# A quarter of the first output rows, stored in whole rows over SP's and GpSimd's queues

## The chip, the cores and the metric

One core of a Trainium2 chip runs the kernel. The metric is the device time of one execution in microseconds, 171.88 us as the median of three runs before the change.

## What is computed

Linear attention without a softmax over 8 batches and 8 heads, a root-mean-square norm of its output, and a soft mixture of 8 experts over the 4608 tokens that come out:

```python
kv = np.einsum('bhsd,bhse->bhde', k, v)
out = np.einsum('bhsd,bhde->bhse', q, kv)
x = out / np.sqrt(np.mean(out * out, axis=-1, keepdims=True) + 1e-06) * g_norm   # as [4608, 512]
logits = x @ phi                                     # [4608, 32]
d = softmax of logits over the tokens;  slot_input = d.T @ x
for e in range(8): slot_out[e] = np.maximum(slot_input[e] @ w1[e], 0) @ w2[e]
return (softmax of logits over the slots) @ slot_out  # [4608, 512]
```

Everything is float32. The inputs are 62 MB, the output 9.4 MB.

## The kernel before

The kernel writes out its own order: every operation is recorded by the class `Order`, with the waits that its operands need, and emitted engine by engine in the order of the program. That is why nearly every row of the profile has one line, L214.

First k, v and q stream in and the attention output is made, token tile by token tile, while the sums over the tokens run along. Then the weights w1 and w2 of the eight experts stream in over the same memory (`arena`), and TensorE makes `expert_h` and `expert_y` as they come. All loads are issued by SP on one queue (q1 in the profile); the last load of weights is issued at 126.46 us.

The output is made in two halves (`hf`) of six chunks each. `output(hf, k, f)` makes chunk n = hf x 6 + k x 2 + f: TensorE multiplies, ScalarE copies one half of the chunk from PSUM into `arena`, VectorE the other half. A chunk is 128 partitions (rows, here) of 1536 floats, 6144 bytes each. `OUT_ROWS` says which chunks are stored together: 0 to 2, 3 to 5, 6 and 7, 8 to 11. The last three stores are one DMA each, over all 128 rows, issued by SP as soon as their last chunk is copied. The first three chunks are stored in pieces by `store_first`, along the table `FIRST`. An entry of it reads: issuing engine, first partition p0, step, number of rows n, length a of the outermost dimension of the destination, number c of pieces that a row is cut into, first chunk k0 and end k1. Each piece goes out as soon as chunk k1 - 1 is there:

- rows 1, 5, 9, ... (every fourth, 32 of them, "the quarter" below): chunk 0 over SP, 30 rows with an outer dimension of 5 (five DMA engines, six rows each) and two rows cut in three; chunk 1 over GpSimd's queue, 24 rows and 8 rows, with an outer dimension of 2 (two engines each); chunk 2 over SP together with rows 3, 7, ...
- rows 3, 7, 11, ...: chunks 0 and 1 over SP, rows of 12288 bytes on all 16 engines
- even rows: chunks 0 to 2 over SP, rows of 18432 bytes on all 16 engines

A DMA that GpSimd issues runs on its own queue, q0. `step_over(n)` is a small copy on that queue, of n rows of 32 bytes from an input into a scrap tile, `stepped`; nobody reads it. Before, there are two of them, of 7 and 6 rows (`STEPS`): the first ahead of the experts, the second between GpSimd's two stores.

The names that the prediction uses: `store_first` and its loop over `FIRST`, `step_over`, `output` with its calls of `store_first` and of the later stores, `load_w`.

Of the kernel before, what the change touches and what calls it, by code (L numbers as in the profile page):

```python
# [11 lines left out]
P = 128  # L12
# [40 lines left out]
OUT_AT = tuple(range(72, 144, 6))  # L53
OUT_ROWS = ((0, 1, 2), (3, 4, 5), (6, 7), (8, 9, 10, 11))
CHUNK = 4 * 12 * 32
FIRST = (
    ("sync", 1, 4, 30, 5, 1, 0, 1), ("sync", 121, 4, 2, 3, 3, 0, 1),
    ("gpsimd", 1, 4, 24, 2, 1, 1, 2), ("gpsimd", 97, 4, 8, 2, 1, 1, 2),
    ("sync", 3, 4, 32, 1, 1, 0, 2), ("sync", 0, 2, 64, 1, 1, 0, 3), ("sync", 1, 2, 64, 1, 1, 2, 3),
)  # L60
STEPS = (7, 6)
SHARED = (5, 11)
HEAD = 144
SCRATCH = 1024
# [212 lines left out]
def first_pieces(out):  # L277

    at = 0
    for _, p0, step, n, a, c, k0, k1 in FIRST:  # L280
        size = (k1 - k0) * CHUNK
        part = out[at : at + n * size]
        rows = part.reshape(n * c // a, a, size // c).swapaxes(0, 1)
        yield p0, step, n, k0, k1, rows.reshape(n, size)
        at += n * size


def soft_moe_linear_attention(nc, first_in, kv_in, q0_in, q1_in, kv4_in, kv5_in, t3_in, w_in, out):
# [12 lines left out]
    def place(at, n):  # L301
        return arena[:, HEAD + at * KB : HEAD + at * KB + n]
# [67 lines left out]
    stepped = const.tile([P, 16], F32, name="stepped")  # L370
# [35 lines left out]
    class Kv:  # L406
# [10 lines left out]
        def products(self, r):  # L417
            g, w = divmod(r, 2)
            main = kv_main(self.b, g).rearrange("p (r w c n) -> p r w c n", r=2, w=2, c=4)
            for c in range(4):  # L420
                for i in range(2):
                    lo = 64 * i
                    nc.tensor.matmul(
                        self.pkv[lo : lo + 64, w, g],
                        lhsT=main[:, w, 1, c, lo : lo + 64],
                        rhs=main[:, w, 0, c, lo : lo + 64],
                        start=c == 0 and (g == 0 or self.b == 0),
                        stop=False,
                    )
# [248 lines left out]
    ends = {starts[s + 1] - 1: s for s in range(len(STAGES))}  # L678
# [46 lines left out]
    for T in range(NT - 2):  # L725
# [3 lines left out]
        o = products(T)  # L729
# [143 lines left out]
    def expert_h(e):  # L873
        ph = ps.tile([P, 2, 512], F32, tag="m", name=f"ph{e}")[:, 0, :256]
        for c in range(4):
            for j in range(4):
                nc.tensor.matmul(
                    ph[32 * j : 32 * j + 32],
                    lhsT=sTe[:, (4 * e + c) * NS : (4 * e + c + 1) * NS],
                    rhs=w_block("w1", e, 4 * c + j),  # L880
                    start=c == 0,
                    stop=c == 3,
                )
        h = wk.tile([P, 256], F32, tag="part", name=f"h{e}", bufs=3)
        nc.scalar.activation(h, ph, AF.Relu, scale=rs)

        x = xts[(NT - 1 - e // 2) % NX].rearrange("p j n -> p (j n)")
        hTs[e] = x[:, e % 2 * 256 : e % 2 * 256 + 256].rearrange("p (c n) -> p c n", n=NS)
        nc.vector.transpose(out=hTs[e].rearrange("p c n -> p (c n)"), in_=h)
# [31 lines left out]
            nc.tensor.matmul(pz[f], lhsT=sel.rearrange("p a n -> p (a n)"), rhs=ys[hf][f], start=True, stop=True)  # L921
        zs[hf] = halves(f"z{hf}", pz)

    def step_over(n):
        ends = [x[:n, : 2 * w].rearrange("p (c n) -> p c n", c=2)[:, :, :4] for x, w in ((stepped, 8), (first_in, 64))]
        nc.gpsimd.dma_start(*ends)

    steps = list(STEPS[::-1])

    def store_first(n):  # L930
        at = 0
        for engine, p0, step, m, a, c, k0, k1 in FIRST:
            size = (k1 - k0) * CHUNK
            if k1 == n + 1:
                src = place(OUT_AT[k0], size)[p0 : p0 + step * (m - 1) + 1 : step]
                dst = out[:, at : at + m * size]
                if c > 1:
                    src = src.rearrange("p (c n) -> p c n", c=c)
                dst = dst.rearrange("o (b a n) -> (o a) b n", a=a, n=size // c)
                getattr(nc, engine).dma_start(dst, src)  # L940
                if engine == "gpsimd" and steps:
                    step_over(steps.pop())
            at += m * size

    def output(hf, k, f):
        z = zs[hf]
        n = (hf * NCH + k) * 2 + f
        at = OUT_AT[n]
        st = place(at, 4 * CT * NS).rearrange("p (a n) -> p a n", a=4)
        shared = n in SHARED  # L950
        for v in range(2):
            fourth = hf == 1 and (2 * n + v) % 4 == 3
            apart = shared and v == 1
            pots = [
                ps.tile([P, 2, 512], F32, tag="y" if y else "m", name=f"po{hf}_{k}_{f}_{v}_{i}", bufs=1 if y else None)
                for i, y in enumerate((False, fourth) if apart else (fourth,))
            ]
            for u in range(2):
                lo = 32 * (2 * v + u)
                po = pots[u if apart else 0]  # L960
                nc.tensor.matmul(
                    po[:, 0 if apart else u, : CT * NS].rearrange("p (g x) -> p g x", g=2),
                    lhsT=z[f][lo : lo + 32],
                    rhs=cT[k][lo : lo + 32],
                    start=True,
                    stop=True,
                )
            if apart:
                nc.vector.tensor_copy(out=st[:, 2], in_=pots[0][:, 0, : CT * NS])
                nc.scalar.copy(st[:, 3], pots[1][:, 0, : CT * NS])  # L970
            elif v == 0:
                nc.scalar.copy(st[:, 0:2], pots[0][:, :, : CT * NS])
            else:
                nc.vector.tensor_copy(out=st[:, 2:4], in_=pots[0][:, :, : CT * NS])
        if n <= OUT_ROWS[0][-1]:
            store_first(n)
        for row in OUT_ROWS[1:]:
            if row[-1] == n:
                lo, m = row[0] * 4 * CT * NS, len(row) * 4 * CT * NS
                nc.sync.dma_start(  # L980
                    out[:, lo * P : (lo + m) * P].rearrange("o (p n) -> (o p) n", p=P), place(OUT_AT[row[0]], m)
                )

    step_over(steps.pop())
    expert_h(0)
    load_w("w2", 3)
    expert_h(1)
# [23 lines left out]
    for k, f in chunks:  # L1011
        output(0, k, f)
# [4 lines left out]
    for k, f in chunks:  # L1017
        output(1, k, f)


def build_program():
    import concourse.bacc as bacc

    nc = bacc.Bacc("TRN2", target_bir_lowering=False, num_devices=1, dynamic_dma_scratch_size=SCRATCH)
    shapes = {
        "first": (P, HEAD + 2304), "kv": (4, P, TOK), "q0": (P, TOK), "q1": (P, 2048),
        "kv4": (P, 2560 + TOK), "kv5": (P, 2 * TOK), "t3": (P, 3 * TOK),
        "w": (1, 2 * NE * P * UNIT),
    }
    args = [nc.dram_tensor(f"in_{n}_dram", s, F32, kind="ExternalInput").ap() for n, s in shapes.items()]  # L1030
    args.append(nc.dram_tensor("out_0_dram", (1, 4 * NCH * P * 4 * CT * NS), F32, kind="ExternalOutput").ap())
    order = Order(nc)
    soft_moe_linear_attention(order, *args)
    order.emit()
    return nc
# [61 lines left out]
```

## Time and profile before

| | us |
|---|---|
| median of 3 runs | 171.88 (171.79 to 171.90) |
| the profiled execution, its own time | 172.04 |
| span of that execution, first to last instruction | 170.70 |
| TensorE busy | 151.3 (89%) |
| VectorE, ScalarE, GpSimd busy | 86.6, 89.0, 59.6 |
| the core's 16 DMA engines | 71.65 MB, 420 GB/s in the mean |

Times in the rows are counted from the start of the span. "DMA share" is the busy share of the 16 DMA engines, q1 is the queue that SP issues to, q0 the one that GpSimd issues to, and an issue's "us to landing" runs from its issue to the last of its engines' reports. A packet is one row or one piece of a row; the packet by which a DMA reports its end on an engine is one of 4 bytes. The execution moves as much data as the DMA engines can for most of its length.

### The profile page before, as it was taken

The numbers are of one execution on the slowest core, as the hardware profiler recorded it, in microseconds if no ns is written. First come the engines' busy times: TensorE is split into PE (matmuls) and PEld (weight loads), VectorE is DVE, ScalarE is ACT, GpSimd is POOL, SyncE is SP. The second block draws the span as 40 slices with busy tenths as digits, with TensorE's granted clock in tenths as the row PEclk, the third lists the DMA queues.
The fourth block names the chain that finished last, engine by engine and source line by source line (L and its number), as shares of the span: only waits on it lengthen the run. The fifth ranks groups of instructions, "written<-read, shape, count | busy, mean of one in ns | idle before, by whom it ended". The sixth has DMA issues, their size and how long they took to land.

```text
span 170.7 us, 4234 instructions
## 1 busy us (share of the span) xinstructions
PE 151.3 (89%) x1832; PEld 105.5 (62%) x1832; DVE 86.6 (51%) x185; ACT 89.0 (52%) x230; POOL 59.6 (35%) x73
## 2 busy tenths in 40 slices
PE   7989697989999899999899998989999989998700
PEld 3469576979778878897697674346665543345300
DVE  1122156284677266762946698823888137205700
ACT  3036576796975886859759864202223045205700
POOL 7000707638357745377382679500000004000000
PEclk9999999999999999999999999999999999699965
DMA  5999999999999999999999999999999999999988
GB/s 190 414 429 423 443 418 440 465 422 454 449 418 434 431 428 430 418 409 449 422 434 422 434 407 426 443 428 420 430 426 438 451 418 407 420 432 410 405 380 369
DMA packets 4365, 71.65 MB, mean 420 GB/s; under 512 B 790, under 2 KB 790, under 8 KB 922
## 3 DMA queue, kind: packets, MB, share of 16 engines
q1 hardware_dynamic: 3994, 71.18, 97.8%
q8 instruction: 14, 0.23, 0.5%
q0 software_dynamic: 352, 0.20, 0.4%
q14 instruction: 5, 0.04, 0.1%
HBM read 61.94 MB, written 9.44 MB: 418 GB/s over the span
## 4 chain that ended last, share of the span: by engine, by line
PE 59%; DMA 13%; ACT 12%; DVE 7%; SPq 2%; issue 1%
PE psum L214 59%; DMA arena<-in_kv_dram 13%; ACT bd L214 3%; ACT sq L214 3%; ACT xall L214 2%; SPq L214 2%; DVE arena L214 1%; DVE logits L214 1%; ACT arena L214 1%; DVE ms L214 1%; ACT part L214 1%; ACT d L214 1%; DVE part L214 1%; ACT r L214 1%; DVE acc L214 1%
## 5 line engine op out<-in xcount | busy, mean ns | idle before, releaser
L214 PE MATMUL psum<-bd,arena 128*128 128x192 f32 (+1 forms) x320 | 56.1, 335 | 1.9 <-ACT bd L214 1.5
L214 PEld LDWEIGHTS psum<-bd,arena 128*128 128x128 f32 (+1 forms) x320 | 45.4, 179 | 8.6 <-ACT bd L214 2.8
L214 DVE TENSOR_REDUCE ms<-sq 128x16 f32<-128x1024 f32 (+1 forms) x19 | 22.1, 1163 | 32.5 <-ACT sq L214 32.3
L214 POOL TENSOR_TENSOR part<-part,r 128x512 f32<-128x512 f32 x17 | 17.8, 1048 | 49.7 <-DVE r L214 49.7
L214 POOL TENSOR_TENSOR xall<-xall,r 128x512 f32<-128x512 f32 x34 | 34.7, 1042 | 0.0
L214 ACT ACTIVATE sq<-psum 128x512 f32<-128x512 f32 x36 | 21.5, 598 | 11.6 <-PE psum L214 11.3
L214 PEld LDWEIGHTS psum<-arena 128*64 128x64 f32 (+1 forms) x640 | 19.0, 137 | 8.3 <-DMA arena<-in_kv_dram 3.2
L214 PE MATMUL psum<-arena 128*64 128x64 f32 (+1 forms) x640 | 21.7, 226 | 2.2 <-DMA arena<-in_kv_dram 2.2
L214 ACT COPY xall<-psum 128x512 f32<-128x512 f32 x34 | 20.6, 606 | 0.0
L214 ACT COPY part<-psum 128x256 f32<-128x256 f32 (+1 forms) x38 | 13.6, 359 | 12.9 <-DVE part L214 11.7
L214 DVE TENSOR_REDUCE logits<-part 128x64 f32<-128x512 f32 (+1 forms) x18 | 17.8, 990 | 0.0
L214 PE MATMUL psum<-arena,xall 128*32 128x256 f32 x256 | 16.4, 411 | 0.0
L214 PE MATMUL psum<-logits,part 32*128 32x384 f32 x96 | 13.5, 524 | 1.5 <-ACT arena L214 0.7
L214 PEld LDWEIGHTS psum<-arena,xall 128*32 128x32 f32 x256 | 8.8, 118 | 7.2 <-issue 2.8
L214 ACT COPY arena<-psum 128x768 f32<-128x768 f32 (+1 forms) x14 | 10.2, 754 | 5.3 <-PE psum L214 5.2
L214 POOL DMA_DIRECT2D out_dram<-arena x2 | 1.2, 592 | 33.4 <-ACT arena L214 33.4
L214 PE MATMUL psum<-arena,sq 128*32 128x256 f32 x224 | 12.7, 379 | 0.2 <-DVE sq L214 0.2
L214 DVE COPY arena<-psum 128x768 f32<-128x768 f32 (+1 forms) x12 | 10.3, 888 | 4.7 <-PE psum L214 4.7
L214 PE MATMUL psum<-xall,d 128*32 128x258 f32 x144 | 10.8, 390 | 0.8 <-ACT d L214 0.8
L214 PEld LDWEIGHTS psum<-logits,part 32*128 32x128 f32 x96 | 6.3, 183 | 7.8 <-ACT arena L214 4.3
L214 ACT COPY bd<-psum 64x128 f32<-64x128 f32 (+1 forms) x32 | 9.9, 309 | 1.6 <-PE psum L214 1.4
L214 PEld LDWEIGHTS psum<-arena,sq 128*32 128x32 f32 x224 | 7.2, 110 | 5.1 <-DVE sq L214 0.5
(80 smaller groups left out, 124.8 us busy)
## 6 DMA issues: line engine op xcount, KB each, us to landing
arena<-in_w_dram SPq DMA_DIRECT2D x4, 4096.0 KB, 23.5
arena<-in_w_dram SPq DMA_DIRECT2D x4, 2048.0 KB, 20.0
arena<-in_t_dram SPq DMA_DIRECT2D x1, 6912.0 KB, 36.0
arena<-in_w_dram SPq DMA_DIRECT2D x2, 3072.0 KB, 22.7
arena<-in_kv_dram SPq DMA_DIRECT2D x2, 2304.0 KB, 23.5
arena<-in_kv_dram SPq DMA_DIRECT2D x1, 4608.0 KB, 42.6
arena<-in_kv_dram SPq DMA_DIRECT2D x1, 3584.0 KB, 32.1
arena<-in_kv_dram SPq DMA_DIRECT2D x3, 1152.0 KB, 12.0
```

Source lines behind the costliest of these rows:

```text
L214: inst = getattr(engine, method)(*args, **kwargs)
```

## The change

The quarter's rows are now stored whole, three chunks at once (18432 bytes), so all pieces of the first three chunks go out when chunk 2 is there. Ten of the 32 rows go over SP, with an outer dimension of 5; 22 go over GpSimd's queue in ten stores: two of three rows, two of four rows with an outer dimension of 2, two of two rows cut in three pieces of 6144 bytes, and four of one row (16 pieces of 1152 bytes each). Between them stand four small copies of 6, 9, 10 and 13 rows (the numbers in `FIRST`). Rows 3, 7, ... now go out whole as well, so the store of chunk 2 alone is gone.

```diff
 FIRST = (
-    ("sync", 1, 4, 30, 5, 1, 0, 1), ("sync", 121, 4, 2, 3, 3, 0, 1),
-    ("gpsimd", 1, 4, 24, 2, 1, 1, 2), ("gpsimd", 97, 4, 8, 2, 1, 1, 2),
-    ("sync", 3, 4, 32, 1, 1, 0, 2), ("sync", 0, 2, 64, 1, 1, 0, 3), ("sync", 1, 2, 64, 1, 1, 2, 3),
+    ("gpsimd", 1, 4, 3, 1, 1, 0, 3), ("gpsimd", 13, 4, 3, 1, 1, 0, 3), ("gpsimd", 25, 4, 4, 2, 1, 0, 3), 6,
+    ("gpsimd", 41, 4, 4, 2, 1, 0, 3), 9, 10, ("gpsimd", 57, 4, 2, 3, 3, 0, 3), 13, ("gpsimd", 65, 4, 2, 3, 3, 0, 3),
+    ("gpsimd", 73, 4, 1, 1, 1, 0, 3), ("gpsimd", 77, 4, 1, 1, 1, 0, 3),
+    ("gpsimd", 81, 4, 1, 1, 1, 0, 3), ("gpsimd", 85, 4, 1, 1, 1, 0, 3),
+    ("sync", 89, 4, 10, 5, 1, 0, 3), ("sync", 3, 4, 32, 1, 1, 0, 3), ("sync", 0, 2, 64, 1, 1, 0, 3),
 )
-STEPS = (7, 6)
+FIRST_STEP = 7
...
-    def step_over(n):
-        ends = [x[:n, : 2 * w].rearrange("p (c n) -> p c n", c=2)[:, :, :4] for x, w in ((stepped, 8), (first_in, 64))]
-        nc.gpsimd.dma_start(*ends)
-
-    steps = list(STEPS[::-1])
-
-    def store_first(n):
-        at = 0
-        for engine, p0, step, m, a, c, k0, k1 in FIRST:
+    def step_over(n, at=0):
+        to = stepped[at : at + n].rearrange("p (c n) -> p c n", c=2)[:, :, :4]
+        nc.gpsimd.dma_start(to, first_in[:n, :128].rearrange("p (c n) -> p c n", c=2)[:, :, :4])
+
+    def store_first():
+        at, steps = 0, 0
+        for x in FIRST:
+            if type(x) is int:
+                steps += 32
+                step_over(x, steps % P)
+                continue
+            engine, p0, step, m, a, c, k0, k1 = x
             size = (k1 - k0) * CHUNK
-            if k1 == n + 1:
...
-                if engine == "gpsimd" and steps:
-                    step_over(steps.pop())
...
-        if n <= OUT_ROWS[0][-1]:
-            store_first(n)
+        if n == OUT_ROWS[0][-1]:
+            store_first()
...
-    step_over(steps.pop())
+    step_over(FIRST_STEP)
```

The end of GpSimd's program before, from the last work on `sq` on (`stepped<-in_first_dram` is a small copy, `out_dram<-arena` a store; the numbers are the destination's dimensions, those of a small copy rows x 2 x 4 floats):

```order
L214 TENSOR_TENSOR xall<-xall,r 128x4x128 x2
L214 MEMSET sq 128x1024
L214 DMA stepped<-in_first_dram 7x2x4
L214 DMA out_dram<-arena 2x12x1536
L214 DMA stepped<-in_first_dram 6x2x4
L214 DMA out_dram<-arena 2x4x1536
```

The same end of GpSimd's program with the change:

```order
L216 MEMSET sq 128x1024
L216 DMA stepped<-in_first_dram 7x2x4
L216 DMA out_dram<-arena 3x4608 x2
L216 DMA out_dram<-arena 2x2x4608
L216 DMA stepped<-in_first_dram 6x2x4
L216 DMA out_dram<-arena 2x2x4608
L216 DMA stepped<-in_first_dram 9x2x4
L216 DMA stepped<-in_first_dram 10x2x4
L216 DMA out_dram<-arena 3x2x1536
L216 DMA stepped<-in_first_dram 13x2x4
L216 DMA out_dram<-arena 3x2x1536
L216 DMA out_dram<-arena 16x1x288 x4
```

Three DMAs behind the first small copy have become fourteen, all behind chunk 2.

The end of SP's program before, from the last load of weights on:

```order
L214 DMA arena<-in_w_dram 128x4096
L214 DMA out_dram<-arena 5x6x1536
L214 DMA out_dram<-arena 3x2x512
L214 DMA out_dram<-arena 32x3072
L214 DMA out_dram<-arena 64x4608
L214 DMA out_dram<-arena 64x1536
L214 DMA out_dram<-arena 128x4608
L214 DMA out_dram<-arena 128x3072
L214 DMA out_dram<-arena 128x6144
```

The same with the change:

```order
L216 DMA arena<-in_w_dram 128x4096
L216 DMA out_dram<-arena 5x2x4608
L216 DMA out_dram<-arena 32x4608
L216 DMA out_dram<-arena 64x4608
L216 DMA out_dram<-arena 128x4608
L216 DMA out_dram<-arena 128x3072
L216 DMA out_dram<-arena 128x6144
```

Five stores of the first three chunks have become three; what follows them is the same. The programs of TensorE, VectorE and ScalarE are the same before and after.

## Rows read from the trace of the kernel before

**Rows 1.** The page: DMA share in 40 slices of the span, and the queues.

```profile
DMA  5999999999999999999999999999999999999988
...
q1 hardware_dynamic: 3994, 71.18, 97.8%
...
q0 software_dynamic: 352, 0.20, 0.4%
```

**Rows 2.** Windows: length, busy time of each engine, TensorE's clock, DMA share, GB/s.

```profile
113.70:137.00 23.30, 23.06 (x417) 13.51 (x416) 13.43 (x33) 4.97 (x11) 0.00 (x0) 1.00 1.02 434
154.00:157.50 3.50, 3.05 (x28) 1.84 (x28) 1.84 (x4) 2.03 (x4) 0.00 (x0) 1.00 1.00 421
157.50:158.70 1.20, 1.20 (x16) 0.68 (x10) 1.05 (x2) 0.93 (x2) 0.00 (x0) 1.00 0.68 292
158.70:162.30 3.60, 2.45 (x18) 1.12 (x16) 2.63 (x4) 2.55 (x4) 0.00 (x0) 1.00 0.99 423
162.30:162.83 0.53, 0.00 (x0) 0.00 (x0) 0.00 (x0) 0.00 (x0) 0.00 (x0) 1.00 0.23 93
```

**Rows 3.** The chain of waits, its end: start us, us, what.

```profile
160.43 0.96 PE psum L214 x4
161.40 0.54 DVE arena L214
```

**Rows 4.** Timeline: start us, us, engine and instruction, of DMA issues and the last copy.

```profile
126.46 0.33 SPq L214 DMA_DIRECT2D arena<-in_w_dram  x1
...
140.23 0.95 SPq L214 DMA_DIRECT2D out_dram<-arena  x1
...
142.27 0.61 POOL L214 DMA_DIRECT2D out_dram<-arena  x1 [33.37 <-ACT arena L214]
142.85 0.51 SPq L214 DMA_DIRECT2D out_dram<-arena  x1
...
142.88 0.56 POOL L214 DMA_DIRECT2D stepped<-in_first_dram  x1
...
147.25 0.36 SPq L214 DMA_DIRECT2D out_dram<-arena  x1
...
161.42 0.48 ACT L214 COPY arena<-psum 128x384 f32<-128x384 f32 x1 [0.34 <-PE psum L214]
162.01 0.33 SPq L214 DMA_DIRECT2D out_dram<-arena  x1
```

**Rows 5.** DMA issues: engine, count, KB, us from issue to landing.

```profile
arena<-in_w_dram SPq DMA_DIRECT2D x1, 2048.0 KB, 23.0
...
out_dram<-arena SPq DMA_DIRECT2D x1, 3072.0 KB, 8.7
```

**Rows 6.** DMA packets that start in 162.30:162.83, and in 162.83:163.20.

```profile
DMA packets 19, 0.05 MB, mean 93 GB/s; under 512 B 15, under 2 KB 15, under 8 KB 15
...
DMA packets 17, 0.39 MB, mean 1063 GB/s; under 512 B 1, under 2 KB 1, under 8 KB 1
```

**Rows 7.** DMA packets that start in 140.00:145.70, and in 145.70:146.10.

```profile
DMA packets 136, 2.41 MB, mean 423 GB/s; under 512 B 16, under 2 KB 16, under 8 KB 16
...
DMA packets 19, 0.15 MB, mean 379 GB/s; under 512 B 7, under 2 KB 7, under 8 KB 11
```

**Rows 8.** DMA queue q0 in 100:120: packets, MB, share of 16 engines.

```profile
q0 software_dynamic: 32, 0.00, 0.1%
```

**Rows 9.** DMA queues in 146:148 and 148:150; packets of 152:154.

```profile
q1 hardware_dynamic: 89, 0.83, 98.1%
q0 software_dynamic: 84, 0.05, 8.0%
...
q1 hardware_dynamic: 75, 0.80, 94.5%
q0 software_dynamic: 74, 0.04, 7.0%
...
DMA packets 171, 0.88 MB, mean 440 GB/s; under 512 B 92, under 2 KB 92, under 8 KB 139
```

More of the change, by code (lines that the diff above doesn't have):

```diff
@@ L279, in first_pieces @@
     at = 0
-    for _, p0, step, n, a, c, k0, k1 in FIRST:
+    for _, p0, step, n, a, c, k0, k1 in (x for x in FIRST if type(x) is tuple):
         size = (k1 - k0) * CHUNK
@@ L922, in mix @@
         zs[hf] = halves(f"z{hf}", pz)
-    def step_over(n):
-        ends = [x[:n, : 2 * w].rearrange("p (c n) -> p c n", c=2)[:, :, :4] for x, w in ((stepped, 8), (first_in, 64))]
-        nc.gpsimd.dma_start(*ends)
-    steps = list(STEPS[::-1])
-    def store_first(n):
-        at = 0
-        for engine, p0, step, m, a, c, k0, k1 in FIRST:
-            size = (k1 - k0) * CHUNK
-            if k1 == n + 1:
[L935 to L940, printed above, removed]
-                if engine == "gpsimd" and steps:
-                    step_over(steps.pop())
+    def step_over(n, at=0):
[9 more added lines that the diff above has]
+            engine, p0, step, m, a, c, k0, k1 = x
+            size = (k1 - k0) * CHUNK
+            src = place(OUT_AT[k0], size)[p0 : p0 + step * (m - 1) + 1 : step]
+            dst = out[:, at : at + m * size]
+            if c > 1:
+                src = src.rearrange("p (c n) -> p c n", c=c)
+            dst = dst.rearrange("o (b a n) -> (o a) b n", a=a, n=size // c)
+            getattr(nc, engine).dma_start(dst, src)
             at += m * size
```

## The prediction, made before the change was run

> **What bounds the kernel now.** I read the page first, then the chain of waits, then the end of the timeline, then windows. The DMA row of the page is nines from the second slice on, so the 16 DMA engines are nearly always at work; only in the last two slices does the share fall to eights [rows 1]. In a full stretch, 113.7 to 137, they move 434 GB/s [rows 2], which is 27.1 GB/s for one engine, so **one row of 18432 bytes takes one engine 0.68 us**. That figure prices everything below.
>
> The end itself is set by compute. The chain of waits from 154 us on runs through TensorE and the copies out of PSUM; its last piece is a copy by VectorE at 161.40 [rows 3], and ScalarE's copy beside it ends at 161.90; then SP issues the last store (four chunks, 3072 KB) at 162.01 [rows 4]. It lands 8.7 us later [rows 5], at 170.7. So the engines wait for the output, not the output for them. The windows say by how much: from 157.50 to 158.70 the DMA share is 0.68, from 162.30 to 162.83 it is 0.23, between them 0.99 [rows 2]. That is 0.32 x 1.20 = 0.38 us and 0.77 x 0.53 = 0.41 us, **0.79 us of idle time per engine in the mean**. It is a mean: at 162.83 one engine was still at the store before. In the window before, 15 closing packets (those under 512 bytes) are counted, and 17 packets start from 162.83 to 163.2, which are 0.39 MB: sixteen rows of 24576 bytes and one closing packet, the sixteenth [rows 6]. So every engine begins the last store within 0.37 us, and the slowest one only costs what it is behind 162.83.
>
> **The change, part by part.** All 32 rows of the quarter (partitions 1, 5, 9, ...) are stored anyway; 576 KB stay 576 KB, 36 KB or 1.36 us per engine in the mean. What changes is when, by whom and on which engines.
>
> *The start.* SP's first store goes out at 140.23 now; with the change it waits for the third chunk, that is for what released the SP store at 142.85 [rows 4]. Cover: the loads of weights. Up to 145.7 the queue moves only large packets (16 under 512 bytes, and as many under 8 KB, so not one row of 6144 bytes); the first such rows are among the 19 packets of 145.7 to 146.1 (11 under 8 KB, 7 under 512 bytes) [rows 7]. A store of SP's reaches the engines 162.83 - 162.01 = 0.82 us after its issue, so the one of 142.85 is there at 143.7, two microseconds before an engine runs out of loads. Cost 0; without that cover an engine would idle for what the store came late, at most 2.62 us (142.85 - 140.23).
>
> *SP.* Five stores become three between 140 and 144.5. SP's next store, at 147.25 [rows 4], waits for a copy, so nothing is gained or lost.
>
> *GpSimd.* Three issues become fourteen (ten stores, four small copies), at 0.56 to 0.61 us each [rows 4]: 7.8 to 8.5 us, from 142.85 to about 151. Nothing stands behind them on GpSimd's program. The copy of 13 rows waits for the first small copy, whose packets are all served by 120 [rows 8]. Cost 0 on the path.
>
> *Small packets.* GpSimd's queue q0 put 352 packets on 16 engines, 22 each [rows 1]. The first small copy is 32 of them, 2 per engine [rows 8]; the other 20 are 13 for 24 rows on two engines (12 and a closing one), 2 and 5. Counted the same way the fourteen are 2+2+3+2+3+2+2+7+2+7+4x2 = 40 per engine, so 20 more. All of q0 took 0.4% of 16 x 170.7 us, 10.9 engine-us; its 0.20 MB of rows are 7.4 of that at 27.1 GB/s, the other 320 packets 0.011 us each. Twenty are **+0.22 us per engine** (0.1 to 0.35, as 0.4% is rounded), less than the 0.79 us that it idles.
>
> *Turns.* While both queues have work, an engine serves one packet of each in turn: 84 of q0 beside 89 of q1 in two microseconds, 74 beside 75 in the next two [rows 9]. From 146 to 157.5 one engine serves 11.5 / 0.68 = 17 large packets, so about 17 of the 40. The two stores of two rows each that stand late in the list (turns 17 to 22 and 26 to 31) then move around 157 to 160, beside or after the gap in SP's queue. They come late, but before 162.8.
>
> *Packet size.* 94 packets of 6144 bytes and 6 of 2048 become 24 of 18432, 12 of 6144 and 64 of 1152. Short rows are no slower here: 152 to 154, with 47 packets between 2 and 8 KB (139 - 92), has 440 GB/s [rows 9], 154.00 to 157.50, with long rows, 421 [rows 2]. Taken as 0; one engine's 36 KB at the one rate or the other differ by 0.06 us.
>
> *Who gets the rows.* This decides. The engines come to the stores at different times: the first short rows start before 146.1, while the last load of weights, issued at 126.46 [rows 4], takes 23.0 us [rows 5] and lands at 149.46. The spread of about 3.4 us is five rows. Unequal shares must fill it. An engine that is late carries 12 KB of the quarter today (its part of the store of chunk 2), 0.45 us. With the change it carries r rows, a sixteenth of four rows (4.5 KB, 0.17 us) and the small packets: 0.68 r + 0.17 + 0.22 - 0.45, which is **-0.06 us for r = 0, +0.62 for one row, +1.30 for two, +2.66 for four**. An early engine may take four (2.7 us) within the spread of 3.4.
>
> On the side of gain: if the shares fit better than now, the slowest engine no longer trails 162.83. That is worth between 0 and 0.37 us [rows 6]; no 12288-byte packet starts after 162.83, so I take the small end, 0.1. On the side of loss the late engine's sum goes up to +2.66.
>
> **Sum.** Unless a late engine is given a full row: 162.01 + 0.82 + 7.84 = 170.67 us for the last landing as now, less 0.1, plus up to 0.3 where an early engine's four rows overfill. The profiled execution was 172.04 us with a span of 170.70; the median of the runs is 171.88, 0.16 lower. So 171.8 to 172.2, and I forecast **171.9**, the same.
>
> **Rivals.**
>
> 1. *A late engine gets rows* (slower). Place: the store of chunks 6 and 7, which that engine ends after 162.83, and from there the last store's rows one for one. It decides from one row on: +0.62 us gives 172.5, two rows 173.2, three 173.9 (1.99), four 174.5. For it: the shares of most engines change, and the trace does not number the engines, so it can't be read there that the late ones are spared. Against it: today's shares are as unequal (by the code 72 KB on two engines, 36 on five, 24 on two, beside 12 on all), and yet the slowest engine is at most 0.37 us behind [rows 6]: a table can fit the engines, so the new one may as well. Chance 0.33.
>
>    One way into it lies in the placement. [...] I hold 0.2 of the 0.33 for the first. [...] No view of this trace shows a copy of three rows.
>
> 2. *The turns* (slower). Should GpSimd's late stores still have rows left when the last store begins, an engine carries 36 KB, 1.36 us, less the 0.79 us it idled: +0.57, 172.5. It decides if fewer than 31 turns are served by 162.8. Against it: the gap at 157.50 empties what holds no rows at once. Chance 0.07.
>
> 3. *A gain over 0.2%* would need nearly all of the 0.37 us [rows 6], or an earlier copy at 161.40, and no compute instruction waits for a store. Chance 0.06.
>
> That leaves 0.54 for the forecast.
>
> **The numbers.** A change of 0.2%, 0.34 us here, is about what a measurement can tell. The forecast lies within it; rivals 1 and 2 beyond it on the slow side, 0.40; the gain 0.06. The forecast's own range is 171.7 to 172.2. For 8 in 10 the range goes from 171.6 to 173.3, which leaves out the larger gain and rival 1 with three rows and more.
>
> **What would show it.** Right: SP's last store issued near 162.0 again and landing 8.7 us later; GpSimd's fourteen issues ending near 151; in the half microsecond before the last store a DMA share as low as now, and 16 first rows within 0.4 us. Rival 1: that share rises in the window before, but the last store lands over 9.2 us after its issue, with the DMA share sinking in its last microseconds, since one engine runs on alone. Rival 2: packets of q0 counted after 162.8. Wrong altogether: a last issue before 161.7 or after 162.4.

## The result, and the profile after

| | before | after |
|---|---|---|
| median, us | 171.84 (171.79 to 171.90, 4 runs) | 173.91 (173.57 to 174.25, 4 runs) |
| ratio | | 1.0117, 95% interval 1.0104 to 1.0130 |
| the profiled execution, its own time | 172.04 | 174.13 |
| span of that execution | 170.7 | 172.8 |

The change makes the kernel 2.07 us slower. That is above the range of the prediction (171.6 to 173.3), whose likeliest case was "the same".

The page of the changed kernel, the rows that answer to [rows 1]: DMA share in 40 slices, and the queues with their packets, MB and share of 16 engines.

```profile
DMA  5999999999999998999999999999999999999992
...
q1 hardware_dynamic: 3887, 70.97, 96.4%
q0 software_dynamic: 672, 0.41, 0.8%
```

The last slice, 4.3 us, falls from eight tenths to two: most engines are done and a few still work. GpSimd's queue has 672 packets instead of 352, 20 more on each engine, as the prediction counted.

The timeline of the changed kernel at the last store: start us, us, what.

```profile
159.69 0.56 DVE L216 COPY arena<-psum 128x384 f32<-128x384 f32 x1 [0.46 <-PE psum L216]
159.73 0.48 ACT L216 COPY arena<-psum 128x384 f32<-128x384 f32 x1 [0.34 <-PE psum L216]
160.32 0.33 SPq L216 DMA_DIRECT2D out_dram<-arena  x1
```

The last store goes out at 160.32 instead of 162.01 [rows 4], 1.69 us *earlier*. What differs there is TensorE's granted clock, and it doesn't take the change for that: e3 below, with the old table, has the higher one as well. The windows of 147 to 150, first the kernel before, then the changed one (length, busy time of PE, PEld, DVE, ACT, POOL, granted clock, DMA share, GB/s):

```profile
147.00:150.00 3.00, 3.00 (x32) 1.43 (x28) 0.00 (x0) 0.22 (x1) 0.00 (x0) 0.50 1.05 438
```

```profile
147.00:150.00 3.00, 3.00 (x64) 1.80 (x57) 0.00 (x0) 0.22 (x1) 3.00 (x7) 1.00 0.99 408
```

Before, the granted clock was 0.50 and 32 matmuls ran in 3 us, after it was 1.00 and 64 did. TensorE was busy for the whole of both windows. Compute is 1.7 us earlier from there on, and the kernel is slower all the same: the first sign that compute doesn't set the end.

The DMA issues of SP's last three stores (chunks 3 to 5, 6 and 7, 8 to 11): count, KB, us from issue to the landing of the slowest engine. Changed kernel, issued at 147.24, 156.18 and 160.32 (the second line is a store of GpSimd's, issued beside the first):

```profile
out_dram<-arena SPq DMA_DIRECT2D x1, 2304.0 KB, 13.6
out_dram<-arena POOLq DMA_DIRECT2D x1, 36.0 KB, 14.7
...
out_dram<-arena SPq DMA_DIRECT2D x1, 1536.0 KB, 9.3
...
out_dram<-arena SPq DMA_DIRECT2D x1, 3072.0 KB, 12.4
```

Before, issued at 147.25 and 157.87 (the last one, 8.7, stands in [rows 5]):

```profile
out_dram<-arena SPq DMA_DIRECT2D x1, 2304.0 KB, 12.4
...
out_dram<-arena SPq DMA_DIRECT2D x1, 1536.0 KB, 5.4
```

Issue and landing added give **three ends**, with which every run below is read: 160.8, 165.5 and 172.7 now, 159.6, 163.3 and 170.7 before. An engine's eight rows of the store of chunks 6 and 7 take 8 x 12288 bytes / 27.1 GB/s = 3.6 us, those of the last store 7.25 us. So now the slowest engine is 1.2 us late at the first end, loses another 1.1 us between the first and the second (4.7 instead of 3.6), and nothing after that (7.2). The trace has the reports of all sixteen engines for the store of chunks 3 to 5: thirteen come by 159.27, the other three at 159.98, 160.13 and 160.84, so only a few engines are late at the first end. The windows of the end say the same (columns as above); they answer to [rows 2].

```profile
157.50:158.70 1.20, 1.05 (x12) 0.41 (x6) 1.05 (x2) 0.89 (x3) 0.00 (x0) 1.00 0.96 366
158.70:162.30 3.60, 0.91 (x4) 0.30 (x4) 1.09 (x2) 1.17 (x2) 0.00 (x0) 1.00 1.03 405
162.30:162.83 0.53, 0.00 (x0) 0.00 (x0) 0.00 (x0) 0.00 (x0) 0.00 (x0) 1.00 1.41 603
162.83:170.20 7.37, 0.00 (x0) 0.00 (x0) 0.00 (x0) 0.00 (x0) 0.00 (x0) 0.51 0.89 384
...
170.20:172.80 2.60, 0.00 (x0) 0.00 (x0) 0.00 (x0) 0.00 (x0) 0.00 (x0) 0.50 0.09 38
```

The two gaps of before (0.68 and 0.23) are filled. But from 157.5 to 162.3 the engines are busy nearly all the time (shares of 0.96 and 1.03) and move 366 and 405 GB/s instead of 434: something makes packets longer. And from 170.2 on they are 9% busy: a few finish alone.

### The profile page after: what moved, and what is told of

The parts are those of the page before. It is cut to its first block, busy times and chain, and to the rows that moved or that the text cites. A ratio compares the mean times of both kernels' runs of the same rounds, so it can differ in the third digit from the quotient of the medians.

```text
span 172.8 us, 4245 instructions
## 1 busy us (share of the span) xinstructions
PE 149.3 (86%) x1832; PEld 105.0 (61%) x1832; DVE 86.7 (50%) x185; ACT 88.9 (51%) x230; POOL 65.7 (38%) x84
## 4 chain that ended last, share of the span: by engine, by line
PE 57%; DMA 13%; ACT 12%; DVE 7%; SPq 2%; issue 1%
PE psum L216 57%; DMA arena<-in_kv_dram 13%; ACT bd L216 3%; ACT sq L216 3%; ACT xall L216 2%; SPq L216 2%; DVE arena L216 1%; DVE logits L216 1%; ACT arena L216 1%; DVE ms L216 1%; ACT part L216 1%; ACT d L216 1%; DVE part L216 1%; ACT r L216 1%; DVE acc L216 1%
## 5 line engine op out<-in xcount | busy, mean ns | idle before, releaser
L216 ACT COPY part<-psum 128x256 f32<-128x256 f32 (+1 forms) x38 | 13.7, 359 | 11.3 <-DVE part L216 10.1
L216 POOL DMA_DIRECT2D out_dram<-arena x10 | 5.5, 551 | 34.3 <-DVE arena L216 34.3
L216 PE MATMUL psum<-arena,xall 128*32 128x256 f32 x256 | 14.8, 380 | 0.1
L216 PEld LDWEIGHTS psum<-arena,xall 128*32 128x32 f32 x256 | 8.3, 110 | 6.1 <-issue 1.1
```

What stands on the lines that cost most here:

```text
L216: inst = getattr(engine, method)(*args, **kwargs)
```

## The experiments

Two theories. **Shares**: the engine with the most rows of the quarter ends last, 0.68 us for each row too many. **Burst**: GpSimd's queue takes time from the engines at the end. The first expectations call the second one "turns" and name a third, "late start": that no store goes out before chunk 2. The medians of before beside the five groups of runs were 171.95 (e1 to e4), 172.00 (e5 to e8), 171.90 (e9 to e12), 171.96 (e13 to e16) and 171.87 (e17, e18).

| run | median, us | ratio, 95% interval | three ends, us |
|---|---|---|---|
| before | 171.9 | | 159.6, 163.3, 170.7 |
| after | 173.91 | 1.0104 to 1.0130 | 160.8, 165.5, 172.7 |
| e1 six rows at one go | 173.43 | 1.0072 to 1.0102 | 160.6, 164.8, 172.1 |
| e3 all behind chunk 2 | 172.00 | 0.9991 to 1.0010 | 159.7, 163.2, 170.4 |
| e4 even shares | 172.64 | 1.0026 to 1.0059 | 160.3, 163.9, 171.1 |
| e5 six rows at one go, own cells | 173.75 | 1.0085 to 1.0121 | 161.3, 165.2, 172.5 |
| e6 eleven copies, late | 173.08 | 1.0048 to 1.0078 | 159.9, 164.5, 171.7 |
| e7 eight stores of three | 175.61 | 1.0194 to 1.0225 | 163.3, 167.0, 174.2 |
| e8 about the old shares | 172.57 | 1.0022 to 1.0046 | 160.4, 164.2, 171.4 |
| e9 nine DMAs | 174.59 | 1.0107 to 1.0213 | 161.8, 165.4, 172.7 |
| e10 twelve copies, early | 172.02 | 1.0000 to 1.0018 | 159.8, 163.4, 170.6 |
| e12 six rows on two engines | 173.87 | 1.0096 to 1.0130 | 161.4, 165.2, 172.7 |
| e13 short pieces | 171.89 | 0.9986 to 1.0006 | 159.6, 163.2, 170.5 |
| e14 e6, short pieces | 172.15 | 1.0003 to 1.0021 | 159.7, 163.4, 170.6 |
| e15 change, short pieces | 173.56 | 1.0077 to 1.0107 | 161.2, 164.9, 172.1 |
| e16 five copies, late | 171.94 | 0.9993 to 1.0012 | 159.5, 163.1, 170.3 |
| e17 e12, short pieces | 173.77 | 1.0059 to 1.0130 | 162.0, 165.6, 172.9 |
| e18 e15, one row less | 172.81 | 1.0040 to 1.0070 | 160.8, 164.4, 171.7 |

**e3, the late start.** The table of before, all of it behind chunk 2:

```diff
-            if k1 == n + 1:
+            if n == OUT_ROWS[0][-1]:
...
-        if n <= OUT_ROWS[0][-1]:
+        if n == OUT_ROWS[0][-1]:
             store_first(n)
```

> The kernel before, with all its pieces of the first three chunks stored when chunk 2 is there; shares, rows and packets are those of before. Theory 'late start': the loss comes with it, 173 to 174. Theories 'shares' and 'turns': 171.84, within 0.1 us, as the loads of weights keep the engines busy until 145.7.

172.00: nothing, so late start is out. Its three issues of SP's last stores, as above:

```profile
out_dram<-arena SPq DMA_DIRECT2D x1, 2304.0 KB, 12.5
...
out_dram<-arena SPq DMA_DIRECT2D x1, 1536.0 KB, 7.0
...
out_dram<-arena SPq DMA_DIRECT2D x1, 3072.0 KB, 10.1
```

Here the clock was 1.00 in 147 to 150 as in the changed kernel; the last store went out at 160.32, 1.7 us earlier than before, and landed at 170.4, only 0.3 us earlier. So **the slowest DMA engine sets the end, not compute**; in the profile of before the two nearly coincided. e3 is also the fair comparison for the change: old shares, same issue times of SP.

**e4, even shares.** The quarter by SP alone, two rows on every engine:

```diff
-    ("gpsimd", 1, 4, 3, 1, 1, 0, 3), ("gpsimd", 13, 4, 3, 1, 1, 0, 3), ("gpsimd", 25, 4, 4, 2, 1, 0, 3), 6,
...
-    ("sync", 89, 4, 10, 5, 1, 0, 3), ("sync", 3, 4, 32, 1, 1, 0, 3), ("sync", 0, 2, 64, 1, 1, 0, 3),
+    ("sync", 1, 4, 32, 1, 1, 0, 3), ("sync", 3, 4, 32, 1, 1, 0, 3), ("sync", 0, 2, 64, 1, 1, 0, 3),
```

> The changed kernel, with the whole quarter stored by SP in one DMA of 32 rows over all 16 engines, two rows each; GpSimd issues the first small copy alone. Theory 'shares': now every late engine has two rows where it had 12 KB, +0.92 us (1.36 - 0.45), less the 20 small packets of before (0.22): about 172.5. Theory 'turns': no packet of GpSimd's is left, so no later than before, 171.8 or less. Theory 'late start': 173.9.

172.64, +0.69, with hardly a packet on GpSimd's queue (32 against 352): by the theory of shares, late engines that carry two rows instead of 12 KB cost that much. Nearly all of it stands in the first end (160.3 against 159.7); the second step is 3.6. As every engine has the same rows here, the reports of the store of chunks 3 to 5 in the trace show how far apart the loads left the engines: from 157.25 to 160.28, 3.0 us.

**e7, where stores of three rows go.** Eight of them in a row:

```diff
-    ("gpsimd", 1, 4, 3, 1, 1, 0, 3), ("gpsimd", 13, 4, 3, 1, 1, 0, 3), ("gpsimd", 25, 4, 4, 2, 1, 0, 3), 6,
...
+    *(("gpsimd", 1 + 12 * i, 4, 3, 1, 1, 0, 3) for i in range(8)), ("sync", 97, 4, 8, 16, 2, 0, 3),
```

> 24 rows of the quarter in eight GpSimd stores of three rows, no small copy between them, the other eight by SP, one each on engines 0 to 7. If a store of three rows always falls on engines 0 to 2, these carry nine rows each beside none on the late engines but 5, 6: the slowest engine lands near 174.4 to 175, median 175.3 to 176.5. If every store goes on where the one before ended, no engine has more than three rows: 172.5 to 173.4.

175.61. The store of chunks 3 to 5 ends 3.6 us later than in e3:

```profile
out_dram<-arena SPq DMA_DIRECT2D x1, 2304.0 KB, 15.8
```

Of the sixteen reports of that store in the trace, thirteen come by 159.47, the other three at 162.32, 162.68 and 163.30. **The eight plain stores of three rows all fell on the same three engines**, eight rows on each; none shifted the place of the next one. No view numbers the engines. The engine numbers in the expectations, and the rows that several stores together put on one engine there (nine here, six in the change), are the author's count from the tables; no run shows it. What e7 does gauge is the slowest engine of the change: it ended the store of chunks 3 to 5 at 160.8, 2.5 us before e7's at 163.3, which is 3.7 rows at 0.68 us. If e7's three engines had the eight rows alone, that leaves 4.3 rows of the quarter, with one of SP's other eight rows on each 5.3: an estimate, and fewer if slow rows (below) have a part in the 160.8.

**e1, e5, e12: the six rows elsewhere.** e1 and e5 put them in one store that divides by three, with a small copy behind it; e12 on two engines. In e5, e6, e8 to e12, e14, e16 and e17 each small copy writes cells of its own:

```diff
-    ("gpsimd", 1, 4, 3, 1, 1, 0, 3), ("gpsimd", 13, 4, 3, 1, 1, 0, 3), ("gpsimd", 25, 4, 4, 2, 1, 0, 3), 6,
+    ("gpsimd", 1, 4, 6, 3, 1, 0, 3), 13, ("gpsimd", 25, 4, 4, 2, 1, 0, 3), 6,     # e1, e5
+    ("gpsimd", 1, 4, 6, 2, 1, 0, 3), 14, ("gpsimd", 25, 4, 4, 2, 1, 0, 3), 6,     # e12
...
-        to = stepped[at : at + n].rearrange("p (c n) -> p c n", c=2)[:, :, :4]
+        to = wk.slots["kvT"][0][:n, at : at + 16].rearrange("p (c n) -> p c n", c=2)[:, :, :4]     # e5, e12
```

> [...] Theory 'shares' (some engines get too many of the 22 rows): six rows change their engine, so the end moves by at least one row, 0.68 us, one way or the other; if the three-row stores were what overfilled the slowest engine (two rows, 1.36 us), about 172.5. Theory 'turns' (the small packets and GpSimd's queue cost it): the same 40 packets per engine within one, so 173.9. Theory 'late start' (no store goes out before chunk 2): 173.9.

> The six rows of the two three-row stores in one store that divides by three, followed by a small copy of 13 rows, and every small copy into cells of its own, so that none waits for an earlier one. If the two stores of the change stood on engines 0, 1 and 2, on top of SP's ten rows (the placement theory), two rows leave the slowest engine, 1.37 us: last landing 171.2 to 171.8 instead of 172.76, median 172.4 to 173.0. If they had been counted on from the place of GpSimd's queue (the rival), the rows of the slowest engine stay as they are: 173.3 to 174.0. If GpSimd's packets themselves cost the time, there are as many as before: 173.6 to 174.2.

> As many GpSimd DMAs as the run with three rows on 7, 8 and 9 (173.75), but the six rows on engines 7 and 8 alone, three each, and 14 rows in the small copy behind them. If a late engine 9 with two rows was what ended last there, what is left is the price of the DMAs: 172.9 to 173.3. If the shares matter no more beside the DMAs' price, 173.6 to 173.9.

173.43, 173.75 and 173.87: none brought the row's worth, and e5 and e12 came where their other theories had them. e1 has a fault of its own, a small copy that waited for an earlier one on the same cells of `stepped` (timeline of e1):

```profile
151.43 0.56 POOL L216 DMA_DIRECT2D stepped<-in_first_dram  x1 [3.72 <-DMA stepped<-in_first_dram]
```

e5 and e12 have not, and are no faster. In e12 the six rows are three each on two engines, and two of its sixteen reports of the store of chunks 3 to 5 come at 161.31 and 161.38, the next at 159.72. What else these two carried isn't shown, so shares may account for that. But something is lost earlier as well. The windows of 146 to 154 (columns as above) of e3, the change, e12 and e9:

```profile
146.00:154.00 8.00, 7.50 (x110) 4.21 (x113) 0.79 (x3) 1.01 (x3) 0.00 (x0) 1.00 1.02 424
146.00:154.00 8.00, 7.50 (x110) 4.21 (x113) 0.79 (x3) 1.01 (x3) 4.86 (x9) 1.00 1.02 417
146.00:154.00 8.00, 7.50 (x110) 4.17 (x113) 0.74 (x3) 1.01 (x3) 4.88 (x9) 1.00 1.02 407
146.00:154.00 8.00, 7.50 (x114) 4.16 (x117) 0.70 (x3) 1.01 (x3) 1.67 (x3) 1.00 1.01 394
```

The engines are as busy and move less. 17 GB/s over 8 us are 0.14 MB, 5.0 engine-us at 27.1 GB/s, more than the 2 x 1.7 by which e12's two engines trail; the change loses 2.1, e9 8.9. e4 and e7 lose nothing there (428 and 424 GB/s). Where few engines bear it, this can add to shares; which ones do, no view shows.

**e2, e6, e10, e11, e16: small copies alone.** The kernel before with more small copies: e2 and e6 eleven behind GpSimd's last store, e16 five there, e10 twelve behind the first one, e11 eleven behind e4's stores.

```diff
             store_first(n)
+        if n == OUT_ROWS[0][-1]:
+            for i in range(11):     # e16: range(5)
+                step_over(8, 16 * i + 32)
...
     step_over(steps.pop())
+    for i in range(12):     # e10, in place of the loop above
+        step_over(8, 16 * i + 32)
```

> The kernel before, with eleven more small copies of 8 rows on GpSimd's queue behind chunk 2: 22 more packets per engine, no row moved. Theory 'turns': most of the loss comes with them, 173 to 174. Theory 'shares': 22 x 0.011 us = 0.24 us per engine at most, of which the slowest engine shows all: 171.8 to 172.1. Theory 'late start': 171.84.

> The kernel before with eleven more small copies behind GpSimd's last store, each into cells of its own, so that GpSimd waits for none. Rows and engines stay those of before. Theory of shares: small packets cost little, 171.8 to 172.2, last landing 170.4 to 170.9. Rival, that the packets and turns of the added DMAs cost what the change lost: 172.8 to 174.

> Twelve small copies of 8 rows as in the run with eleven, but right behind the first one, ahead of the experts, while only loads of weights are under way; rows and engines of the kernel before. If a GpSimd DMA takes its time from the DMA engines wherever it stands, 172.9 to 173.3 again. If its price belongs to the end, where it meets the store of chunks 6 and 7, 171.8 to 172.2.

> The even shares by SP alone (172.64) and eleven small copies behind them. If the price of GpSimd's DMAs and that of the shares add up, 172.64 + 1.08: 173.5 to 174.0. If the small copies only delay engines that are early, 172.5 to 172.9.

The kernel keeps its waits by blocks of 32 rows of a tile, and e2's copies of 8 rows share such blocks of `stepped`, so nine of the eleven waited for an earlier one and they outlasted the kernel (185.69, ratio 1.0822): it says nothing of a burst. e6, without these waits, took **173.08**, 1.08 us more, with the rows where they were before. e10, twelve copies at 108 to 115 us, took 172.02: next to nothing (1.0000 to 1.0018). In e11 the copies had nothing ahead of them on GpSimd's program and went out at 108 as well; 172.76 (1.0036 to 1.0066) beside e4's 172.64 repeats e10. So it isn't the packets but *when* they are served. e6's three issues:

```profile
out_dram<-arena SPq DMA_DIRECT2D x1, 2304.0 KB, 12.6
...
out_dram<-arena SPq DMA_DIRECT2D x1, 1536.0 KB, 8.3
...
out_dram<-arena SPq DMA_DIRECT2D x1, 3072.0 KB, 11.4
```

The first end is e3's, 159.9 to 159.7; the second comes 4.6 us later instead of 3.5. Nearly all of the loss lies between the two. The DMA queues from 158.5 to 160, e6 and then e3 (packets, MB, share):

```profile
q1 hardware_dynamic: 50, 0.50, 91.8%
q0 software_dynamic: 176, 0.00, 6.6%
```

```profile
q1 hardware_dynamic: 58, 0.59, 92.6%
q0 software_dynamic: 1, 0.00, 0.0%
```

GpSimd's packets are short, 6.6% of 16 x 1.5 = 24 engine-us, over 176, is 0.009 us each, but there are 3.5 of them to one of SP's, no longer one to one as in [rows 9], and SP's rows beside them take 0.918 x 24 / 0.50 = 44 us per MB instead of e3's 37.7. One packet each, in windows of 2 ns (share x 16 x 0.002 us is its duration): a row of 12288 bytes that starts amid that burst in e6 (at 159.256), and a normal one in the changed kernel.

```profile
q1 hardware_dynamic: 1, 0.01, 3456.2%
```

```profile
q1 hardware_dynamic: 1, 0.01, 1437.5%
```

1.11 us against 0.46. The reading: while one store of SP's is under way, an engine takes packets of the two queues in turn; at the end of it, what GpSimd's queue still holds is served in one go, and single rows beside it take more than twice their time. Most of the rows there still took 0.46, and why the others are slow isn't shown.

> The kernel before with five small copies behind GpSimd's last store instead of eleven. If each costs the same tenth of a microsecond: 172.4 to 172.6. Theory of the burst: an engine has some 6 free turns in the store of chunks 3 to 5 and serves 10 packets more, so a burst of some 4 is left: 172.0 to 172.3.

Five copies cost nothing (171.94): most of their packets fit between SP's, and 42 of GpSimd's are left in 158.5 to 160 instead of e6's 176. The price isn't a tenth for each copy; it sets in somewhere between five and eleven.

**e13, e14, e15: more turns.** The test of that reading: the store of chunks 3 to 5 in pieces of 6144 bytes, 24 packets per engine instead of 8 ahead of the boundary, in the kernel before (e13), in e6 (e14) and in the change (e15):

```diff
-                nc.sync.dma_start(
-                    out[:, lo * P : (lo + m) * P].rearrange("o (p n) -> (o p) n", p=P), place(OUT_AT[row[0]], m)
-                )
+                c = len(row) if row == OUT_ROWS[1] else 1
+                dst = out[:, lo * P : (lo + m) * P].rearrange("o (c p n) -> (o p) c n", p=P, c=c)
+                nc.sync.dma_start(dst, place(OUT_AT[row[0]], m).rearrange("p (c n) -> p c n", c=c))
...
```

> Control: the kernel before, with the store of chunks 3 to 5 in pieces of 6144 bytes instead of rows of 18432, three times as many packets of SP's queue ahead of the store of chunks 6 and 7. GpSimd's queue is short here and served before that: 171.7 to 172.2 by every theory.

> The same, with the eleven small copies behind GpSimd's last store (173.08 with long rows). Theory of the burst: what GpSimd's queue still has when an engine ends the store of chunks 3 to 5 is served there in one go and costs 1.0 us; with 24 turns instead of 8 in that store most of its packets go one by one between SP's, which costs nothing, so 171.8 to 172.4. Rival, that these packets cost their time wherever they are served late: 172.9 to 173.3.

> The change, with the same pieces of 6144 bytes in the store of chunks 3 to 5. Theory of the burst: the part of its loss that is burst goes, 0.5 to 1 us, and the part that is shares (an engine with six rows of the quarter) stays: 172.9 to 173.5. If all of its loss is shares: 173.7 to 174.1. If all were burst: 171.9 to 172.3.

e13 171.89, e14 **172.15** where the same copies cost 173.08: 0.93 of the 1.08 us are gone. e14's queues from 158.5 to 160, and its issue of the store of chunks 6 and 7:

```profile
q1 hardware_dynamic: 77, 0.67, 105.5%
q0 software_dynamic: 31, 0.00, 1.2%
...
out_dram<-arena SPq DMA_DIRECT2D x1, 1536.0 KB, 7.3
```

31 packets of GpSimd's are left there instead of 176. So the price of e6 hangs on what GpSimd's queue still holds at the boundary: the burst is shown. In the change (e15) the second step falls from 4.7 to 3.7, but the first end comes at 161.2 instead of 160.8:

```profile
out_dram<-arena SPq DMA_DIRECT2D x1, 2304.0 KB, 13.9
out_dram<-arena POOLq DMA_DIRECT2D x1, 36.0 KB, 10.6
...
out_dram<-arena SPq DMA_DIRECT2D x1, 1536.0 KB, 8.7
...
out_dram<-arena SPq DMA_DIRECT2D x1, 3072.0 KB, 11.8
```

A GpSimd store of two rows that is issued beside SP's (36 KB) now lands after 10.6 us instead of 14.7: its rows come before the boundary and no longer behind it, so a part of the loss may only move from the second step into the first. The gain is 0.35 us, less than expected and hardly clear of noise (the intervals of e15 and of the change just overlap); 1.6 us are left.

**e18, e17: what is left.** In the trace of the change SP's store of ten rows, issued at 142.84, has six reports, one at 144.15 and five from 147.81 to 150.65, which fits two rows each on five engines. e18 is e15 with these rows on ten engines, one each; e17 is e12 with the short pieces.

```diff
-    ("sync", 89, 4, 10, 5, 1, 0, 3),
+    ("sync", 89, 4, 10, 10, 1, 0, 3),     # e18
```

> The change with pieces of 6144 bytes in the store of chunks 3 to 5 (173.56), and SP's ten rows one each on engines 0 to 9 instead of two each on 0 to 4: GpSimd's queue is the same, engines 0 to 4 carry one row less, 5 to 9 one more. Theory of shares: one row, 0.68 us, off the slowest engines: 172.7 to 173.1. If engines 5 and 6 or 9, late ones, become the slowest, not under 172.7. If shares are not what is left, 173.4 to 173.8.

> The six rows of the two three-row stores on engines 7 and 8 (173.87 with long rows), and the store of chunks 3 to 5 in pieces of 6144 bytes. If the change's remaining loss with short pieces (173.56) is the six rows that engines 0 and 2 carry, it falls by at least one row: 172.2 to 172.9. If bursts at the earlier boundaries of SP's stores, between the rows of chunks 0 to 2, have taken their place, 173.2 to 173.9 again.

e18 172.81: one row less on each of SP's five engines gives 0.75 us in the medians (0.5 in the profiled executions), where 0.68 was a row's price. **One row of what is left is shares.** The last 0.94 us weren't divided: they stand in the first end (e18's is 160.8, e3's 159.7), where shares that are left and slow rows as in 146 to 154 above aren't told apart. e17 stayed at 173.77 with a wide spread. Two rows of 18432 bytes of GpSimd's in it, again in windows of 2 ns, at 150.01 and 151.50:

```profile
q0 software_dynamic: 1, 0.02, 4668.8%
...
q0 software_dynamic: 1, 0.02, 4796.9%
```

1.49 and 1.53 us where 0.68 is normal. That fits bursts at the earlier boundaries, between SP's stores of chunks 0 to 2, and might explain e5 and e12 too, but it wasn't tested. The longest row of e15 took 1.55 us as well, and in 146 to 154 e9, with fewer DMAs of GpSimd's, loses more than e12, where e7, with as many as e9, loses nothing. So what makes rows slow there stays open.

**e8, e9: whole rows in other splits.** e8 has about the old shares, as the author counted them, with few GpSimd DMAs, e9 the change's rows over nine DMAs instead of fifteen:

```diff
...
+    ("gpsimd", 1, 4, 12, 2, 1, 0, 2), 6, ("gpsimd", 49, 4, 4, 3, 3, 0, 2), ("sync", 1, 4, 16, 1, 1, 2, 3),     # e8
+    ("gpsimd", 65, 4, 1, 1, 1, 0, 3), ("sync", 69, 4, 15, 5, 1, 0, 3),
...
+    ("gpsimd", 1, 4, 8, 2, 1, 0, 3), 6, ("gpsimd", 33, 4, 4, 2, 1, 0, 3), 9, 10, ("gpsimd", 49, 4, 2, 3, 3, 0, 3), 13,     # e9
+    ("gpsimd", 57, 4, 2, 3, 3, 0, 3), ("sync", 65, 4, 3, 1, 1, 0, 3), ("sync", 77, 4, 3, 1, 1, 0, 3),
+    ("sync", 89, 4, 10, 5, 1, 0, 3),
```

> Everything behind chunk 2 and nearly all rows in long pieces, as in the change, but engines loaded about as before the change: 4 1/3 rows on engines 7 and 8, 3 on 15, 3 1/3 on 0 to 4, 1/3 on the rest. Theory of shares: 171.6 to 172.1. Rival, that long rows that all start behind chunk 2 are what costs: 172.8 to 174.

> The rows of the change over nine GpSimd DMAs instead of fifteen (the first small copy counted): the two stores of three rows go over SP, in the same form, and the four single rows join the first store on engines 7 and 8. [...] If a GpSimd DMA costs 0.1 us, as the eleven copies alone did (1.08 us), six fewer give 173.1 to 173.5. If only the shares count, the slowest engine loses its quarter row: 173.5 to 173.8. If SP's three rows fall elsewhere than GpSimd's did, more.

e8 172.57, between the two expectations: its second step is 3.8, hardly a burst, and its first end 0.7 us late; by the tables SP's five engines carried 3 1/3 rows of the quarter where the old ones are 2 2/3, an estimate from the rows of each store and the five reports (before's store of 30 rows has five as well, from 147.54 to 149.51). It also moves 405 GB/s in 146 to 154, so shares and slow rows aren't told apart there. e9 fell wide (173.46 to 175.33). In its profiled execution the first end, 161.8, holds nearly the whole loss and the second step is 3.6: without a burst at that boundary, but with the largest loss in 146 to 154, it ends as late as the change. Why other executions of it took longer stays open.

No run beat the kernel before: e13 and e16 equal it.

## Why the prediction was wrong

- *"The end itself is set by compute."* Wrong. e3 issued the last store 1.7 us earlier and landed 0.3 us earlier. The 0.79 us of idle time, against which small packets and overfilled engines were set off, were thus hardly a reserve: e4's engines, 0.6 us late at the first end, cost 0.69 us. The sum should have been made for the slowest engine's rows, not for the last copy.
- *The start*, *SP*, *GpSimd* (issues to about 151; the last one ends at 150.86): right, cost 0; e3 shows the first.
- *Small packets.* The count of 20 more per engine was right, the price wrong, +0.22 us at 0.011 us a packet. Early they cost nothing (e10), late, and in a burst, 1.08 us for 22 (e6; 176 in 158.5 to 160 are 11 an engine in the mean).
- *"Turns"*, rival 2, had the place but not the size: "the gap at 157.50 empties what holds no rows at once". In the profiled execution there was no gap, since the clock held and SP's store came at 156.18; and what is emptied at once is not free. Its sign, packets of q0 after 162.8, is there (15), but 200 of them start in 158.5 to 160.
- *"Packet size. Taken as 0."* Perhaps wrong, by way of the turns: SP's stores of the first three chunks have 106 rows and pieces where they had 196, so fewer turns in which GpSimd's packets pass unnoticed. For these stores it wasn't tested by itself; e14 shows it from the other side, for the store of chunks 3 to 5.
- *Who gets the rows*, **the step that failed**: "plus up to 0.3 where an early engine's four rows overfill". The term, put at 0.3 at most, measured 1.1 us at the first end against e3, with slow rows perhaps in it; a row more or less is worth 0.75 (e18). e7's gauge gives the slowest engine 4.3 to 5.3 rows, 2.9 to 3.6 us at 0.68, where the spread was 3.4 by the prediction's reading and 3.0 by e4's reports. Whether it was an early engine at all isn't shown. The prediction held 0.2 for stores of three rows that go round the engines. No run shows that; in e7 all eight fell on the same three, a pile that the prediction left out. By e18 the engines that end last have rows of SP's ten as well; whether they are the same three isn't shown.
- Rival 1's 173.9 for three rows meets the 173.91 by luck: its sum for a late engine with three rows has no burst in it. The second term that the sum lacked is the burst. Against e3 the profiled execution lost 1.1 us before the first end and 1.2 between the first and the second. The medians divide it by what was taken away: 0.35 us for the short pieces (e15), 0.75 for one row (e18), and 0.94 left.

What the prediction named as its own refutation, "a last issue before 161.7", came true, but by the clock: e3 has it too and loses nothing. Of rival 1's signs, the landing over 9.2 us after the issue is in e3 as well (10.1); the share that sinks at the end (0.09 from 170.2 on) is the one that tells the change.

## What to carry to other kernels

When DMA engines are full, give each engine its own account: when it is done with what came before, the rows that each store puts on it, and which stores fall on the same engines each time. The end of compute in the same profile may only coincide with theirs, so move it (or look at a run in which it moved) before taking it for the bound. Small DMAs of a second queue were free here as long as the first queue offered a packet for nearly each of them (e10, e14, e16); count the first queue's packets up to the next boundary between its stores against what the second queue still holds, and cut the rows shorter if they don't suffice.

## What the runs showed of the hardware

- Where both queues had work within a store, they were served one packet to one (84 beside 89, 74 beside 75 in [rows 9]). At the end of a store of SP's, in e6, 176 packets of GpSimd's went through beside 50 of SP's in 1.5 us, and a row beside them took 1.11 us instead of 0.46 (12288 bytes). Rows of GpSimd's of 18432 bytes took up to 1.5 us instead of 0.68 at 150 to 152 in e17. No run here shows the cause of either.
- A small copy that the kernel lets wait for an earlier one waits for its report: 3.72 us in e1, and 1.35 to 13.03 us in e2, the last of them at 184.19.
- TensorE's clock in 147 to 150 was 0.50 in the profile of before and 1.00 in those of the change and e3, under the same work. TensorE was busy for the whole of that stretch in each. It moved the last store by 1.7 us and the span by 0.2 (170.7 to 170.5).
